# A GELU MLP on one core: the order of a small copy and the turning of a bias on VectorE

## The chip, the cores and the metric

The kernel runs on one core of a Trainium2 chip. The metric is the device time of one execution in microseconds (us). A profile of one execution is a little shorter than that time (93.8 us against 95.05 us for the profiled run of the kernel before); its span runs from the first recorded instruction to the last. Engines are named as in the profile: PE is TensorE's matmuls, PEld its weight loads, DVE is VectorE, ACT ScalarE, POOL GpSimd, SP SyncE.

## The reference

```python
B, S, D, F = 1, 2048, 448, 1792          # all tensors bf16
h = einsum("bsd,df->bsf", x, w1) + b1
h = gelu(h, approximate=True)
out = einsum("bsf,fd->bsd", h, w2) + b2
```

The contraction of layer 1 has 448 = 3 x 128 + 64 rows. The last 64, the remainder rows, are the subject here.

## The kernel before

Every matmul of the two layers uses 64 of the 128 rows of the array, upper half or lower half by turns, and the halves work side by side. A pair of output tiles (`lo` = 0 and 1) goes through part a (three blocks, 64 rows of each) and part b (the other 64 rows of these blocks, then the remainder). In the last step of part b, tile 0 uses the upper half and tile 1 the lower, so the remainder rows of w1 of every odd tile must lie in the lower 64 partitions. The DMA brings them to the upper ones, and an engine copies them down. A helper records every operation and puts the semaphore waits that its list `after` names. The bias b1 arrives as 14 rows of 128 and is turned by VectorE, with four transposes and a cast (a copy into another type).

```python
RCUTS = (0, 4, 14)            # remainder rows come as tiles 0-3, then 4-13
def turn_b1():
    for q in range(4):
        pr.op("vector", ... e.transpose(b1t[32*q:32*q+32, :], b1n[:, 32*q:32*q+32]) ...)
    pr.op("vector", ... e.tensor_copy(b1_f, b1t[:, 0:NFT]) ..., event="b1")
...
# Layer1.step, k == KT (the remainder):
lhsT = w1r[rows, ft*P:(ft+1)*P]
after = [("w1r" if half else "w1rU", int(ft >= RCUTS[1]))]   # half 0 needs the copy
...
L[0].a(0, HC)
turn_rest()                   # TensorE turns the rest of x, VectorE and ScalarE copy it out
turn_b1()
for i in (0, 1):
    odd = ...                 # the odd tiles' columns of block i
    pr.op("vector", ... e.tensor_copy(odd(slice(0, H)), odd(slice(H, P))),
          after=[("w1r", i)], event=("w1rU", i))
L[1].a(0, HC); L[0].a(HC, SC); L[1].a(HC, SC)
L[0].b(); L[1].b(); L[2].a()
for j in range(3, NPAIR):
    L[j].a(); L[j - 1].b()
```

The gelu of a pair, on ScalarE, needs the turned bias and empties the pair's PSUM unit (PSUM is the memory that holds the sums of the matmuls). There are four units, so the fifth pair of layer 1 waits for the gelus of the first.

Of the kernel before, what the change touches and what calls it, by code (L numbers as in the profile page):

```python
# [73 lines left out]
def bass_standalone__dense_activation_gelu__prompt_kernel(  # L74
# [23 lines left out]
    with ExitStack() as es:  # L98
# [80 lines left out]
        def turn_b1():  # L179
            for q in range(4):  # L180
                pr.op("vector", lambda e, q=q: e.transpose(  # L181
                    b1t[32 * q:32 * q + 32, :], b1n[:, 32 * q:32 * q + 32]), after=["b1n"], event=("b1t", q))
            pr.op("vector", lambda e: e.tensor_copy(b1_f[:, :], b1t[:, 0:NFT]),  # L183
                  after=[("b1t", q) for q in range(4)], event="b1")
# [187 lines left out]
        def turn_rest():  # L372


            turn_block(1, 2, 2, 0, [("xT0", 0, 2)])
            for q in range(STC // 2):
                turn(lambda half, q=q: spot(2, 1)[:, half, q, :], lambda rows, q=q: xr[rows, q, :], ("xr", q), ["xr_in"])
            drain_blocks("vector", 1, (2,), 2, ("xr", 1))
            for src, engine in enumerate(("vector", "scalar")):
                i = spot(2, 1, HALVES[src])  # L380
                for dst in (src, 1 - src):
                    o = xT[HALVES[dst], KT, 0:SC].rearrange("p (q two b s) -> p b q two s", q=2, two=2, b=2)[:, :, :, src, :]
                    pr.op(engine, lambda e, o=o, i=i, engine=engine:
                          e.copy(o, i) if engine == "scalar" else e.tensor_copy(o, i),  # L384
                          after=[("xr", 1), ("xT0", 1, 2)], event=("xR0", dst, src))
            busy[(2, 1)] = ("xR0", 1, 0)
            busy[(2, 2)] = ("xR0", 0, 1)
# [4 lines left out]
        L = [Layer1(0, j) for j in range(NPAIR)]  # L392
        L[0].a(0, HC)
        turn_rest()
        turn_b1()

        for i in (0, 1):
            odd = lambda rows, i=i: w1r[rows, RCUTS[i] * P:RCUTS[i + 1] * P].rearrange(
                "p (j two q) -> p j two q", two=2, q=P)[:, :, 1, :]
            pr.op("vector", lambda e, odd=odd: e.tensor_copy(odd(slice(0, H)), odd(slice(H, P))),  # L400
                  after=[("w1r", i)], event=("w1rU", i))
        L[1].a(0, HC)
        L[0].a(HC, SC)
        L[1].a(HC, SC)
# [70 lines left out]
```

## Time and profile before

| | before |
|---|---|
| time, median of 3 runs (range) | 94.79 us (94.73 to 94.97) |
| span of the profile | 93.8 us |
| TensorE busy | 90.0 us, 96% |
| VectorE busy | 13.4 us, 14% |
| TensorE idle for the copy of remainder rows | 0.64 us as shown |

The rows of the profile that carry these are in the prediction below. Read such a profile in this order: which engine the chain that ended last runs through, where that chain leaves the engine, and then the timeline of each engine around that place.

### The profile page before, as it was taken

The page shows a single profiled execution, that of the slowest core. Times are in us where ns is not written, and L with a number is a line of the kernel's source. Part 1 is how long each engine was busy: PE and PEld are TensorE (multiplying, and loading weights), DVE is VectorE, ACT ScalarE, POOL GpSimd, SP SyncE. Part 2 cuts the span into 40 slices and gives each one's busy share as a digit, 9 for nine tenths or more (in the row PEclk, how much of TensorE's full clock was granted, in tenths as well). Part 3 has the DMA queues.
Part 4 walks back from the last instruction along what each step waited for, and adds up shares of the span by engine and source line. Part 5 has one row for each costly group of instructions (what it writes and reads, how often), then busy time and mean ns, then how long its engine had stood idle before and what let it go on. Part 6 is the DMA issues. An engine that isn't in the chain of part 4 may idle for free.

```text
span 93.8 us, 2086 instructions
## 1 busy us (share of the span) xinstructions
PE 90.0 (96%) x945; PEld 50.3 (54%) x945; DVE 13.4 (14%) x34; ACT 38.5 (41%) x64; POOL 1.7 (2%) x8
## 2 busy tenths in 40 slices
PE   6997999999999999999999999999999999999990
PEld 2382444566664444566654444566654444576990
DVE  0156001100234000000235000000134000000421
ACT  6065687900002887900001878900001878910001
POOL 6000000000000000000000000000000000000000
PEclk9999999999999999999999999999999999999999
DMA  2999999745564000000033000000022000000022
GB/s 47 347 278 323 380 294 114 130 102 119 73 136 155 0 0 7 0 0 0 0 99 104 0 3 0 7 0 0 0 98 98 7 0 0 0 0 7 24 74 98
DMA packets 12744, 7.32 MB, mean 78 GB/s; under 512 B 6976, under 2 KB 12544, under 8 KB 12736
## 3 DMA queue, kind: packets, MB, share of 16 engines
q1 hardware_dynamic: 11904, 6.80, 29.6%
q10 hardware_dynamic: 800, 0.39, 1.4%
q8 instruction: 7, 0.11, 0.5%
q14 instruction: 1, 0.01, 0.0%
q0 software_dynamic: 32, 0.00, 0.0%
HBM read 3.79 MB, written 1.84 MB: 60 GB/s over the span
## 4 chain that ended last, share of the span: by engine, by line
PE 94%; DVE 2%; issue 1%; ACT 0%; DVEq 0%
PE u L217 89%; PE u L192 4%; PE u L344 1%; DVE b1t L181 1%; DVE xT L384 1%; ACT out_sb L329 0%; DVE xT L357 0%; DVE w1r L400 0%; DVE b_f L183 0%; DVEq L63 0%
## 5 line engine op out<-in xcount | busy, mean ns | idle before, releaser
L269 ACT ACTIVATE g<-u,b_f 128x512 bf16<-128x512 f32 x56 | 35.0, 684 | 40.0 <-PE u L217 38.9
L217 PE MATMUL u<-w_sb,g 64*128 64x448 bf16 (+1 forms) x504 | 43.9, 328 | 0.0
L217 PE MATMUL u<-xT,w_sb 64*128 64x512 bf16 (+1 forms) x348 | 43.5, 371 | 0.1
L217 PEld LDWEIGHTS u<-w_sb,g 64*128 64x128 bf16 x504 | 28.7, 94 | 14.1
L217 PEld LDWEIGHTS u<-xT,w_sb 64*128 64x128 bf16 x348 | 19.5, 95 | 19.1 <-DMA w_sb<-in_w_dram 0.2
L217 PE MATMUL u<-xT,w1r 64*128 64x512 bf16 x56 | 16.7, 376 | 0.6 <-DVE w1r L400 0.6
L312 DVE TENSOR_TENSOR out_sb<-u,b_bc 128x448 bf16<-128x448 f32 x14 | 8.1, 620 | 61.3 <-PE u L217 61.3
L217 PEld LDWEIGHTS u<-xT,w1r 64*128 64x128 bf16 x56 | 5.3, 94 | 4.5 <-DVE w1r L400 1.1
L329 ACT CAST out_sb<-u 128x224 bf16<-128x224 f32 x1 | 0.3, 345 | 9.3 <-PE u L217 9.3
L192 PE MATMUL u<-const-bfloat16-1.0 128*128 128x512 bf16 (+1 forms) x8 | 3.4, 601 | 0.8 <-PEq L460 0.8
L192 PEld LDWEIGHTS u<-const-bfloat16-1.0 128*128 128x128 bf16 x8 | 1.0, 140 | 2.4 <-issue 2.4
L357 ACT COPY xT<-u 128x256 bf16<-128x256 bf16 x3 | 1.0, 374 | 2.5 <-PE u L344 2.5
L175 ACT ACT_TABLE_LOAD x1 | 1.3, 1283 | 0.7 <-PEq L460 0.7
L344 PEld LDWEIGHTS u<-ident,xn 64*128 64x128 bf16 x24 | 0.9, 127 | 0.9 <-issue 0.8
L187 DVE COPY xT<-xT 64x512 bf16<-64x512 bf16 x3 | 0.9, 289 | 3.4 <-DMA xT<-in_x_dram 3.3
L344 PE MATMUL u<-ident,xn 64*128 64x64 bf16 x24 | 1.1, 238 | 0.1
L423 DVE COPY b_z<-b_bc 1x448 bf16<-1x448 bf16 x1 | 0.3, 268 | 5.8 <-DMA b_bc<-in_b_dram 5.8
L384 ACT COPY xT<-u 64x256 bf16<-64x256 bf16 x2 | 0.7, 368 | 0.9 <-DVE xT L357 0.8
L357 DVE COPY xT<-u 128x256 bf16<-128x256 bf16 x3 | 0.8, 292 | 1.2 <-PE u L344 1.2
L320 DVE TENSOR_TENSOR out_sb<-u,b_bc 128x448 bf16<-128x448 f32 x1 | 0.6, 625 | 1.8 <-PE u L217 1.8
L181 DVE STREAM_TRANSPOSE b1t<-b1n 32x32 bf16<-32x32 bf16 x4 | 0.8, 202 | 0.1
L362 DVE COPY xr<-xn 128x256 bf16<-128x256 bf16 x1 | 0.2, 227 | 3.2 <-DMA xn<-in_x_dram 3.2
(18 smaller groups left out, 4.8 us busy)
## 6 DMA issues: line engine op xcount, KB each, us to landing
out_dram<-out_sb SPq DMA_DIRECT2D x16, 112.0 KB, 1.7
w_sb<-in_w_dram SPq DMA_DIRECT2D x2, 784.0 KB, 8.3
w_sb<-in_w_dram SPq DMA_DIRECT2D x1, 576.0 KB, 6.0
xn<-in_x_dram SPq DMA_DIRECT2D x1, 448.0 KB, 3.4
w_sb<-in_w_dram ACTq DMA_DIRECT2D x2, 192.0 KB, 4.1
w_sb<-in_w_dram SPq DMA_DIRECT2D x1, 384.0 KB, 4.5
xT<-in_x_dram SPq DMA_TRANSPOSE x12, 3.8
w1r<-in_w_dram SPq DMA_DIRECT2D x1, 160.0 KB, 4.8
```

What stands on the lines that cost most here:

```text
L175: pr.op("scalar", lambda e: e.activation(junk[:, :], one, ACT.Gelu_apprx_tanh), event="table")
L181: pr.op("vector", lambda e, q=q: e.transpose(b1t[32 * q:32 * q + 32, :], b1n[:, 32 * q:32 * q + 32]), after=["b1n"], event=("b1t", q))
L187: pr.op("vector", lambda e: e.tensor_copy(xT[0:H, KT, s0:s1], xT[H:P, KT, s0:s1]), after=after, event=event)
L192: pr.op("tensor", lambda e: e.matmul(unit[0][:, 0, 0:cols], lhsT=ones_w, rhs=ones_m[:, 0:cols], start=True, stop=True))
L217: o = pr.op("tensor", lambda e: e.matmul(unit[u][:, lo, cols], lhsT=lhsT, rhs=rhs, start=start, stop=stop, skip_group_check=skip), after=a ...
L269: pr.op("scalar", lambda e, lo=lo, ft=ft: e.activation(g[:, ft, c * SC:(c + 1) * SC], unit[u][:, lo, :], ACT.Gelu_apprx_tanh, bias=b1_f[:, ...
L312: pr.op("vector", lambda e, lo=lo, j=j: e.tensor_tensor(out=out_sb[:, j, :], in0=unit[u][:, lo, 0:D], in1=b2_bc[:, :], op=ALU.add), after= ...
L320: pr.op("vector", lambda e: e.tensor_tensor(out=out_sb[:, j, :].rearrange("p (two h) -> p two h", two=2), in0=unit[u][:, :, 0:DH], in1=b2_ ...
L329: pr.op("scalar", lambda e: e.copy(out_sb[:, j, DH:D], unit[u][:, 1, 0:DH]), after=[y[1]], event=("o", j, 1))
L344: pr.op("tensor", lambda e, half=half, rows=rows: e.transpose(o(half), i(rows), ident[rows, rows]), after=["ident"] + after, event=event i ...
L357: pr.op(engine, lambda e, i=i: (e.copy if engine == "scalar" else e.tensor_copy)(o[:, i], f[:, i]), after=[wait or ("xt", h, ks[-1])], eve ...
L384: e.copy(o, i) if engine == "scalar" else e.tensor_copy(o, i),
```

## The change

The first copy of remainder rows (tiles 0 to 3) goes ahead of the five instructions that turn the bias. The intent is that TensorE, which needs that copy first, waits for it no longer. The second copy stays last.

```diff
         L[0].a(0, HC)
         turn_rest()
-        turn_b1()
 
         for i in (0, 1):
             ...
             pr.op("vector", lambda e, odd=odd: e.tensor_copy(odd(slice(0, H)), odd(slice(H, P))),
                   after=[("w1r", i)], event=("w1rU", i))
+            if i == 0:
+                turn_b1()
```

## The prediction

> **What bounds the kernel now.** I read the page first (busy shares, then the chain that ended last), then the chain in order of time, then the timeline of each engine around the one gap in it.
>
> ```profile
> PE 90.0 (96%) x945; PEld 50.3 (54%) x945; DVE 13.4 (14%) x34; ACT 38.5 (41%) x64; POOL 1.7 (2%) x8
> PE 94%; DVE 2%; issue 1%; ACT 0%; DVEq 0%
> ```
>
> TensorE (PE) sets the time: 94% of the chain that ended last is its matmuls. VectorE (DVE) is busy for 14% of the span but holds 2% of that chain, about 2 us, so there is one place where TensorE waits for it. The chain in order of time says where (start us, length us, what):
>
> ```profile
> 6.75 0.28 DVE xT L384
> 7.03 0.03 issue
> 7.07 0.20 DVE b1t L181
> ...
> 7.76 0.22 DVE b1t L181
> ...
> 8.10 0.18 DVE b_f L183
> 8.27 0.03 issue
> 8.30 0.23 DVE w1r L400
> 8.54 0.05 issue
> 8.59 82.99 PE u L217 x868
> ```
>
> From 6.11 to 8.54 us the chain runs through VectorE alone: it finishes turning x (L384), transposes the bias (L181, four times), casts it (L183), and only then copies the first remainder rows of w1 to the lower 64 partitions (L400). From 8.59 on the chain is one unbroken run of 868 matmuls up to the last output. So whatever moves the point 8.59 forward moves the end, unless a later wait appears in that run. What TensorE did meanwhile (two answers of the timeline, matmuls and weight loads, start, length, shapes, idle before and releaser):
>
> ```profile
> 7.57 0.38 PE L217 MATMUL u<-xT,w1r 64*128 64x512 bf16 x1
> 8.59 0.39 PE L217 MATMUL u<-xT,w1r 64*128 64x512 bf16 x1 [0.64 <-DVE w1r L400]
> 7.36 0.09 PEld L217 LDWEIGHTS u<-xT,w1r 64*128 64x128 bf16 x1
> 8.58 0.09 PEld L217 LDWEIGHTS u<-xT,w1r 64*128 64x128 bf16 x1 [1.13 <-DVE w1r L400]
> ```
>
> The first matmul on the remainder rows reads the rows as the DMA left them (upper half) and runs at 7.57. Its partner reads the copied rows (lower half) and runs at 8.59, released by the copy. The idle time of 0.64 us is only from the modelled end of one matmul to the start of the next; the loss in the rhythm of starts is larger, as worked out below.
>
> **What the Trainium skill says.** (1) "TensorEngine Tiling (Array Packing)", section Key Properties: tiles are independent, and different tiles can load weights and multiply in parallel. All matmuls here use 64 of 128 rows. The trace agrees: the groups of two remainder matmuls in layer 1 start at 11.40 and 12.91, and 14 matmuls lie between those points, so 1.51 / 14 = 0.108 us each, or one pair every 0.216 us. (2) "TensorE: Matmul & The Clock Gate", section Back-to-back issue gap, gives N/2.4 + 2.5 ns for the warm array, which is 216 ns for 512 columns; the pair rhythm just found is that, so two half-row streams each run at the full column rate. (3) "VectorE: DVE Perf Modes", section Two Vector instructions with no wait between them: an instruction whose inputs or output start in another group of 32 partitions than the ones before waits until every earlier one has finished. The trace agrees: L400's two copies, alike in partitions, overlap (0.22 + 0.35 us of work in 0.49 us), while the unlike neighbours in the chain above are 0.03 us apart. (4) "Perfetto Trace Analysis", section Tensor Engine Instruction: matmul ends in a profile are estimated. Hence I reckon with starts.
>
> **The change part by part.** Nothing is added or removed: five VectorE instructions of the bias (4 transposes, 1 cast) and one copy change places. In both orders the second copy (the other ten blocks of w1) comes last.
>
> The copy. After the last L384 ends at 7.03 it starts at about 7.06 and takes 0.23, so it is done at 7.29; with the 0.05 from copy to weight load that the chain shows, TensorE may go on at 7.34 instead of 8.58. Its own input landed long before: issued at 2.26, 3.7 us to landing, so 5.96.
>
> TensorE. Its pairs before the stop follow at 7.13, 7.35, 7.57, so the partner would have run beside the matmul at 7.57. ScalarE's last copy of x, which that partner needs too, ends at 6.49 + 0.76 = 7.25, also in time. So the partner moves from 8.59 to 7.57 or a hair later (its half of the array: 1.02 us earlier) and the next pair from 8.59 to 7.57 + 0.22 = 7.79 (the other half, whose first matmul of that pair now starts at 8.59: 0.80 us earlier). The half that gains only 0.80 is the later one from then on: before, one half was a matmul behind the other, afterwards they march level.
>
> The bias. It is ready not at 8.28 but one copy and one gap later, at 8.28 + 0.26 = 8.54. ScalarE's first gelu therefore starts at about 8.63 instead of 8.37.
>
> The second copy. It loses the overlap with the first and ends at about 8.57 + 0.35 = 8.92 instead of 8.79.
>
> The end. The last store waits for a VectorE sum (91.51 + 0.39 = 91.90) fed by the half that gains 0.80, and for a ScalarE copy (91.60 + 0.34 = 91.94) fed by the half that was a matmul behind. The first becomes 91.10; the second catches up and ends before it. So the store is released 91.94 - 91.10 = 0.84 us earlier. Sum: 94.79 - 0.84 = 93.95 us, or 0.9% less.
>
> **The rivals.**
>
> Rival 1, a later bias becomes the new wait. These rows are ScalarE's in the timeline:
>
> ```profile
> 8.37 2.56 ACT L269 ACTIVATE g<-u,b_f 128x512 bf16<-128x512 f32 x4 [1.11 <-DVE b_f L183]
> 11.82 1.26 ACT L269 ACTIVATE g<-u,b_f 128x512 bf16<-128x512 f32 x2 [0.89 <-PE u L217]
> ```
>
> ScalarE waits for the bias, and TensorE wants the four PSUM units back. The fifth pair of layer 1 takes the first unit again; it starts now at 8.59 + 14 pairs x 0.216 = 11.6, and will at 10.8. Its unit is free after two gelus, which begin at 8.63 and take 0.64 each in the row above, plus the tail of the last: 10.0. Slack 0.8 us. The four first gelus end at 11.19 instead of 10.93, and the third pair's, wanted by then at 11.0, is late by 0.2; a pair takes ScalarE 1.27 and TensorE 1.51, so ScalarE is level again one pair later. The 0.89 us that ScalarE idles before 11.82 speaks for this too. If I am wrong here, TensorE would stop at the fifth pair and the time would be between 94.0 and 94.8.
>
> Rival 2, a transfer takes the place of the wait. SyncE's issues in the timeline, and microseconds to landing from the list of DMA issues:
>
> ```profile
> 2.26 0.55 SPq L137 DMA_DIRECT2D w1r<-in_w_dram  x1
> 2.87 0.57 SPq L130 DMA_DIRECT2D w_sb<-in_w_dram  x1
> 3.48 0.50 SPq L137 DMA_DIRECT2D w1r<-in_w_dram  x1
> 4.02 0.59 SPq L130 DMA_DIRECT2D w_sb<-in_w_dram  x1
> ```
>
> ```profile
> w_sb<-in_w_dram SPq DMA_DIRECT2D x1, 576.0 KB, 6.0
> w_sb<-in_w_dram SPq DMA_DIRECT2D x1, 384.0 KB, 4.5
> w1r<-in_w_dram SPq DMA_DIRECT2D x1, 160.0 KB, 4.8
> w1r<-in_w_dram SPq DMA_DIRECT2D x1, 64.0 KB, 3.7
> ```
>
> The 384 KB of w1 land at 2.87 + 4.5 = 7.4; the third pair wants them after 4 pairs of matmuls, at 7.79 + 4 x 0.216 = 8.65. The 576 KB land at 4.02 + 6.0 = 10.0; the fifth pair wants them at 10.8. The other remainder rows land at 8.3 and their copy ends at 8.92; they are wanted at about 10.6. w2 was issued from 4.65 with 8.3 us to landing, thus about 13 to 14.5, and layer 2 will want it at 16.2 instead of 17.02. No transfer is within 0.7 us of binding. The DMA is near full in this stretch, so a run in which the 576 KB are late by more than 0.8 would lose part of the gain: 94.1 to 94.6.
>
> Rival 3, only the size differs. If the end follows the 0.64 us of shown idle time, the time is 94.15; if it follows the half of the array that gains 1.02, it is 93.77. If the copy came a few hundredths too late for the slot at 7.57 (it has about 0.2 us), the partner would slip and the lag of one half would stay; still at least 0.6 us would be won.
>
> Rival 4, the clock. The page grants full speed in all 40 slices (row PEclk), the matmul at 7.57 lasts as long (0.38) as the later ones, so there is no slow clock that the pause causes and its removal would lift.
>
> **Range and chances.** 93.95 us is the sum; the other sizes span 93.77 to 94.15, and the three runs of before lie 0.24 us apart, so I take 93.70 to 94.25 for eight in ten. Faster by over 2% would need less than 92.9, a gain of 1.9 us, which is more than the whole wait: 1%. Slower by over 2% has no mechanism here: 1%. Within 2%: 98%.
>
> **What would show it.** In the changed profile: L400's first copy starts at 7.06 and the four transposes follow at 7.33; the wait of TensorE for DVE w1r L400 is gone from the list of waits; both matmuls on the remainder rows of the first pair start at 7.57 to 7.6; the unbroken run of matmuls starts before 8 us, and VectorE's share of the chain falls from 2% to about 1%; the first gelu starts near 8.63 after a wait of 1.4 for the bias; layer 2 begins near 16.2. I am wrong if TensorE shows a new wait for w_sb, for ScalarE or for the second copy between 8 and 14 us, or if the first gelu's delay is still seen at layer 2's start.

## The result, and the profile after

The changed kernel takes 94.15 us (median of 6 runs, 93.69 to 94.43); the kernel before, in the same rounds and those of its first measurement, 94.94 us (94.73 to 95.06). The ratio is 0.9915 with a 95% interval of 0.9886 to 0.9945, so the gain is 0.8%, some 0.81 us. Ratios here are the mean time of one kernel's fast runs over that of the other's fast runs of the same rounds, so not quite the ratio of the medians quoted. Every execution behind a ratio in this document was in the fast state.

The page of the changed kernel, the chain by engine and by line:

```profile
PE 92%; DMA 4%; DVE 1%; issue 0%
PE u L217 92%; DMA xn<-in_x_dram 4%; DVE out_sb L326 0%; PE u L344 0%; DVE xT L357 0%
```

The lines for the bias (b1t) and for the copy (w1r) are no longer in the chain. Its pieces in order of time show one run of matmuls to the end, now from 5.64 us instead of 8.59:

```profile
5.64 84.80 PE u L217 x903
90.44 0.38 DVE out_sb L326
```

VectorE's timeline: the copy (L399 now) follows directly on the last copies of x, then the bias, and the second copy waits for its transfer:

```profile
6.02 0.60 DVE L384 COPY xT<-u 64x256 bf16<-64x256 bf16 x2
6.66 0.22 DVE L399 COPY w1r<-w1r 64x256 bf16<-64x256 bf16 x1
6.91 0.90 DVE L181 STREAM_TRANSPOSE b1t<-b1n 32x32 bf16<-32x32 bf16 x4
7.95 0.18 DVE L183 CAST b_f<-b1t 128x14 f32<-128x14 bf16 x1
9.20 0.35 DVE L399 COPY w1r<-w1r 64x640 bf16<-64x640 bf16 x1 [1.07 <-DMA w1r<-in_w_dram]
```

TensorE's timeline: the two remainder matmuls of the first pair are now one group, both starting at 7.28, since the group lasts 0.38, which is the length of one. The next pair follows 0.22 us later, in the next slot (a slot is a pair's place in the rhythm of starts, 0.216 us long):

```profile
7.28 0.38 PE L217 MATMUL u<-xT,w1r 64*128 64x512 bf16 x2
7.50 0.81 PE L217 MATMUL u<-xT,w_sb 64*128 64x512 bf16 x6
```

The span falls by 93.8 - 92.6 = 1.2 us, more than the time does. The part of it that the change did not make can be read off: VectorE was done with x at 6.02 + 0.60 = 6.62 in this execution and at 7.03 in the one of before, with the same instructions up to there. What that is, the second traces show.

### The profile page after: what moved, and what is told of

Same layout as the page of the kernel before. It is cut to its first block, busy times and chain, and to the rows that moved or that the text cites. A ratio compares the mean times of both kernels' runs of the same rounds, so it can differ in the third digit from the quotient of the medians.

```text
span 92.6 us, 2086 instructions
## 1 busy us (share of the span) xinstructions
PE 89.1 (96%) x945; PEld 45.6 (49%) x945; DVE 13.5 (15%) x34; ACT 38.4 (41%) x64; POOL 1.7 (2%) x8
## 4 chain that ended last, share of the span: by engine, by line
PE 92%; DMA 4%; DVE 1%; issue 0%
PE u L217 92%; DMA xn<-in_x_dram 4%; DVE out_sb L326 0%; PE u L344 0%; DVE xT L357 0%
## 5 line engine op out<-in xcount | busy, mean ns | idle before, releaser
L217 PE MATMUL u<-w_sb,g 64*128 64x448 bf16 (+1 forms) x504 | 43.2, 328 | 0.0
L217 PE MATMUL u<-xT,w_sb 64*128 64x512 bf16 (+1 forms) x348 | 41.0, 369 | 0.3 <-DVE xT L357 0.2
L217 PEld LDWEIGHTS u<-w_sb,g 64*128 64x128 bf16 x504 | 24.5, 94 | 18.4
L217 PEld LDWEIGHTS u<-xT,w_sb 64*128 64x128 bf16 x348 | 16.7, 94 | 19.6 <-DMA w_sb<-in_w_dram 1.0
L217 PE MATMUL u<-xT,w1r 64*128 64x512 bf16 x56 | 10.6, 376 | 0.0
L217 PEld LDWEIGHTS u<-xT,w1r 64*128 64x128 bf16 x56 | 2.7, 94 | 3.3
L192 PE MATMUL u<-const-bfloat16-1.0 128*128 128x512 bf16 (+1 forms) x8 | 3.2, 577 | 0.8 <-PEq L461 0.8
L192 PEld LDWEIGHTS u<-const-bfloat16-1.0 128*128 128x128 bf16 x8 | 1.0, 137 | 2.4 <-issue 2.4
L399 DVE COPY w1r<-w1r 64x256 bf16<-64x256 bf16 (+1 forms) x2 | 0.6, 289 | 1.1 <-DMA w1r<-in_w_dram 1.1
```

The costliest lines, as they stand in the source:

```text
L192: pr.op("tensor", lambda e: e.matmul(unit[0][:, 0, 0:cols], lhsT=ones_w, rhs=ones_m[:, 0:cols], start=True, stop=True))
L217: o = pr.op("tensor", lambda e: e.matmul(unit[u][:, lo, cols], lhsT=lhsT, rhs=rhs, start=start, stop=stop, skip_group_check=skip), after=a ...
L399: pr.op("vector", lambda e, odd=odd: e.tensor_copy(odd(slice(0, H)), odd(slice(H, P))), after=[("w1r", i)], event=("w1rU", i))
```

## The experiments

All gave correct results. In the tables "before" is the kernel before in the same rounds.

| run | what | median us | before us | ratio (95%) |
|---|---|---|---|---|
| again | the changed kernel | 93.97 | 94.93 | 0.9908 (0.9874 to 0.9942) |
| fine_after | changed, last block of w1 in two transfers | 93.85 | 94.93 | 0.9908 (0.9876 to 0.9939) |
| fine_before | before, with that split | 94.62 | 94.93 | 0.9982 (0.9952 to 1.0012) |
| pool_copy | before, first copy on GpSimd | 93.97 | 94.93 | 0.9920 (0.9884 to 0.9957) |
| copy_mid | copy after two transposes | 94.09 | 94.67 | 0.9933 (0.9905 to 0.9961) |
| copy_k4 | copy after four transposes, ahead of the cast | 94.45 | 94.67 | 0.9978 (0.9956 to 1.0000) |
| bias_last | both copies ahead of the bias | 95.16 | 94.67 | 1.0043 (1.0006 to 1.0081) |
| delay6 | changed, bias 1.3 us later | 94.33 | 94.67 | 0.9956 (0.9931 to 0.9981) |

Four more were single looks, for their traces: copy_k3 (94.61 us), copy_mid_again (94.05), before_again (94.44) and after_third (93.74), with a single run of the kernel before at 94.84. Single runs have no known state and carry no verdict, and none is drawn from their times.

My theory was that the whole gain is TensorE's wait for the copy, and that the bias and the transfers have room to spare. The rivals: the later bias is what moves the time; the transfers of w1 are the new wait; TensorE waits as a whole rather than half by half.

### The copy on another engine, the bias where it was (pool_copy)

```diff
-            pr.op("vector", lambda e, odd=odd: e.tensor_copy(...),
-                  after=[("w1r", i)], event=("w1rU", i))
+            pr.op("gpsimd" if i == 0 else "vector", lambda e, odd=odd: e.tensor_copy(...),
+                  after=[("w1r", i)] + (["ident", "b2z0"] if i == 0 else []), event=("w1rU", i))
```

The added waits are on GpSimd's own earlier instructions. The author added them because the check for races refused the kernel without them; the record keeps no trace of that refusal.

> The kernel before, with the first copy of remainder rows done by GpSimd, which is idle from 2.5 us on, in place of VectorE; the bias stays first on VectorE. My theory (TensorE waited for the copy, whatever engine makes it, and the delay of the bias neither helps nor hurts): if GpSimd is done with it by 7.5 us, the gain is that of the changed kernel, ratio 0.991 to 0.992, with ScalarE's first gelu at about 8.1 to 8.3 as in the kernel before less one copy. Rival (the later bias is what changed the time, by moving ScalarE's work): no gain from this kernel, ratio 0.998 to 1.002. If GpSimd takes over 1.5 us for the copy, the gain is smaller by what it is late.

GpSimd's timeline, and then TensorE's at the first pair:

```profile
5.92 0.39 POOL L400 COPY w1r<-w1r 64x256 bf16<-64x256 bf16 x1 [3.44 <-DMA w1r<-in_w_dram]
```

```profile
7.21 0.38 PE L217 MATMUL u<-xT,w1r 64*128 64x512 bf16 x2
```

The copy is done at 6.31, the two remainder matmuls again start together, and the ratio is that of the changed kernel (0.9920 against 0.9915 and 0.9908). The bias is ready at 7.93 and ScalarE's first gelu starts at 8.03, without the copy in front. So the gain is the copy's coming in time, on either engine, and it needs no move of the bias. A copy done 0.9 us ahead of its use, as here, gains nothing over one done 0.4 us ahead, as in the changed kernel.

### How late the copy may be (copy_mid, copy_k4, copy_k3, copy_mid_again)

```diff
         turn_rest()
+        turn_b1(range(n), False)          # n = 2, 3 or 4 transposes, no cast
         for i in (0, 1):
             ...
             if i == 0:
-                turn_b1()
+                turn_b1(range(n, 4))      # the rest, and the cast
```

> The changed kernel with the copy after two of the four transposes of the bias. The copy is then done 0.46 us later, at about 7.75 in the clock of the profile of before, 0.2 us after the slot of its matmul. My theory (two half-row streams; only the half that needs the copy slips, the other half's next matmul waits no longer than about 7.80 against 7.79): one half falls a matmul behind again but the end moves by at most 0.05 us, ratio 0.991 to 0.993. Rival (TensorE as a whole waits for the copy from the moment the first matmul of its pair starts): 0.2 us of the gain lost, ratio 0.993 to 0.995.

> The changed kernel with the copy after all four transposes but ahead of the cast. The copy is done about 8.24 and TensorE goes on at about 8.29 in place of 8.59 in the kernel before. My theory: 0.30 us less than before, ratio 0.996 to 0.998, and TensorE again shows a wait for the copy, of 0.7 to 0.8 us for its weight load. Rival (the order alone matters, or the bias's cast): either the full gain, 0.991 to 0.992, or none.

> The changed kernel with the copy after three of the four transposes; one look for the trace. From VectorE's last copy of x to TensorE's release the chain should be 3 x 0.233 + 0.25 + 0.05 = 1.0 us; the slot of the partner matmul lay 0.5 to 0.9 us after that copy in the traces so far. My theory (two half-row streams): the partner starts at the release, 0.1 to 0.5 us after its slot, while the next matmul of the other half starts at the later of the release and 0.22 us after the slot; from that next matmul to the last drain it is 83.35 us, as in the kernel before, and not 83.29, as in the changed kernel, since one half is a matmul behind. Rival (both halves wait alike): the next pair starts 0.22 us after the late partner.

> The kernel with the copy after two transposes again, one look: in its first trace TensorE's slow clock lasted until 6.6 us and its slot came so late (0.95 us after VectorE's last copy of x) that the copy was in time, and the run told nothing. If the clock rises earlier this time, the slot is 0.5 to 0.7 us after that copy, the release 0.77 after it, the partner 0.1 to 0.25 us late, and the other half's next matmul not late at all or by less than 0.05 (my theory); the rival has it late by as much as the partner.

With four transposes ahead, the wait is back. The chain of copy_k4:

```profile
7.44 0.23 DVE w1r L401
7.67 0.05 issue
7.72 82.99 PE u L218 x868
```

From VectorE's last copy of x (its end at 6.47) to the release at 7.72 it is 1.25 us, against 1.56 in the kernel before (7.03 to 8.59): the 0.31 us that the cast and the waits before it cost, which is the expected 0.30. The time agrees (ratio 0.9978, within the 0.996 to 0.998 expected).

The first run of copy_mid told nothing. TensorE itself was slow in its trace: the first remainder matmul started only 0.95 us after the last copy of x, at 7.85, so the copy, done at 7.62, was in time. Its ratio of 0.9933 has an interval that holds both theories. The second look caught the case. TensorE's timeline of copy_mid_again, and then that of copy_k3:

```profile
7.30 0.64 PE L218 MATMUL u<-xT,w1r 64*128 64x512 bf16 x2
7.56 1.03 PE L218 MATMUL u<-xT,w_sb 64*128 64x512 bf16 x6
```

```profile
7.65 0.87 PE L218 MATMUL u<-xT,w1r 64*128 64x512 bf16 x2
8.13 0.60 PE L218 MATMUL u<-xT,w_sb 64*128 64x512 bf16 x3
```

A group of two lasts from the start of the first to the end of the second, so the partner starts 0.64 - 0.38 = 0.26 us after the first matmul in copy_mid_again and 0.87 - 0.38 = 0.49 after it in copy_k3. The next matmul, on the other half, starts at the same moment as the late partner, not a slot of 0.22 us behind it. In copy_mid_again it is therefore at 7.56 where it would have been at 7.30 + 0.22 = 7.52: the partner lost 0.26 us, the other half 0.04. The rival of a TensorE that waits as a whole would have put it at 7.78. The halves are two streams, but they start in the order of TensorE's one list: the next matmul needs nothing of the copy, and in all six traces with a late partner it starts 3 or 4 ns after that partner, never ahead of it. So the other half loses what the partner is late, less one slot: 0.04 us of 0.26 here, 0.27 of 0.49 in copy_k3, and 0.80 of 1.02 in the kernel before. That is why a copy which one half alone needs held up both. From that next matmul to the last drain (the copy of the last sums out of PSUM) copy_k3 took 83.35 us, as expected of a kernel with one half behind.

### How late the bias may be (delay6, bias_last)

```diff
             if i == 0:
+                for q in range(6):        # delay6: into a buffer that nothing reads
+                    pr.op("vector", ... e.transpose(b1d[...], b1n[...]) ...)
                 turn_b1()
```

```diff
-            if i == 0:
-                turn_b1()
+        turn_b1()                         # bias_last: after the loop
```

> The changed kernel with six more transposes of the bias into a buffer that nothing reads, between the copy and the bias: 6 x 0.233 = 1.4 us more, so that the bias is ready at about 9.9 in the clock of before (9.35 in that of the changed kernel's profile), and the first pair's gelus end at 11.4 (10.75). My theory (0.8 us of slack): TensorE waits for the PSUM unit ahead of the fifth pair and loses 0.4 to 0.6 us against the changed kernel, ratio 0.995 to 0.998. If the slack is larger than 1.4, ratio 0.991 to 0.992; if there is none, 1.004 to 1.007.

> The changed kernel with the bias after both copies. The second copy waits for its transfer, which landed at 8.3 in the trace of before and at 9.2 in that of the changed kernel, so the bias is ready only at about 9.9 to 10.8 and the first pair's two gelus end at 11.3 to 12.1. My theory (bias has 0.8 us of slack and no more, since the fifth pair of layer 1 wants the first PSUM unit back at 10.6 to 10.8): TensorE waits for ScalarE there, and 0.5 to 1.5 us are lost against the changed kernel: ratio 0.997 to 1.007. Rival (the time of the bias does not matter at all): ratio 0.991 to 0.992.

The chain of delay6 at the place that the expectation named:

```profile
9.33 1.28 ACT g L270 x2
10.60 0.14 issue
10.74 79.89 PE u L218 x849
```

TensorE's remainder matmuls of the third pair started at 10.06, so the fifth pair's turn was at 10.06 + 0.22 = 10.28, and it started at 10.74: 0.46 us lost, where 0.4 to 0.6 was expected. By the times, 0.9956 against the changed kernel's 0.9908 to 0.9915 is 0.4 to 0.5% of 94.7 us, again 0.4 to 0.5 us; but those ratios come from other rounds and their intervals overlap, so it is the trace that shows the loss. In this trace the bias could have come 0.46 us sooner than 9.24, so at 8.78, without loss; in the changed order without the 1.3 us it would have been ready at about 7.95. That is the 0.8 us of room that the prediction reckoned.

In bias_last the second copy waits for its transfer (landing at 8.77), the bias comes at 10.38, and TensorE's row for the fifth pair reads:

```profile
11.89 0.61 PE L217 MATMUL u<-xT,w_sb 64*128 64x512 bf16 x4 [1.36 <-ACT g L269]
```

Its turn was at 10.15 + 0.22 = 10.37, so 1.52 us are lost, and the kernel is slower than the one before (1.0043). So the 0.25 us by which the changed order delays the bias lie within its room, and a delay of more than 0.8 us does not.

### The transfers (again, fine_after, fine_before)

```diff
-        W1CUTS = (0, 2, 4, 8, 14)
+        W1CUTS = (0, 2, 4, 8, 10, 14)
...
         load_w1(3)
+        load_w1(4)
```

> The changed kernel itself, once more, for a second trace and a tighter interval. My theory (the whole gain is that TensorE no longer waits for the copy of the first remainder rows): 0.80 to 0.84 us less than before, a ratio of 0.991 to 0.992, and no wait of TensorE for the copy. Rival (transfers of w1 are the new wait in many runs, so that part of the gain is lost and the times scatter): 0.3 to 0.7 us less, ratio 0.993 to 0.997, and a wait of TensorE for the 384 KB or the 576 KB of w1 of more than 0.1 us in the trace.

> The changed kernel with the last block of w1 (tiles 8 to 13) loaded as two transfers, tiles 8 and 9 first, so that the fifth pair's weights land about 1 us earlier. If the transfers cost the changed kernel nothing on average (my theory): the same time as the changed kernel within 0.1 us, ratio to before 0.990 to 0.993. If the landing of this block has become the wait in many runs (rival): up to 0.3 us faster than the changed kernel and a smaller scatter, ratio 0.987 to 0.989.

> The kernel before with that same split of the last block of w1. Here TensorE wants the fifth pair's weights about 0.8 us later, so neither theory expects a gain: ratio 0.997 to 1.003. A gain as large as in the run of the split on the changed kernel would say that the split helps for another reason than the one under test.

The first trace of the changed kernel showed weight loads that waited for a transfer (PEld, with idle time before and releaser):

```profile
8.33 1.64 PEld L217 LDWEIGHTS u<-xT,w_sb 64*128 64x128 bf16 x18 [0.30 <-DMA w_sb<-in_w_dram]
10.55 0.55 PEld L217 LDWEIGHTS u<-xT,w_sb 64*128 64x128 bf16 x8 [0.36 <-DMA w_sb<-in_w_dram]
```

Most of that idle time is not TensorE's: a weight load runs ahead of its matmul (the one at 7.36 in the kernel before belongs to the matmul at 7.57). The first matmul behind the second wait started at 10.56, and its turn was at 10.30 + 0.22 = 10.52, so 0.04 us were lost; behind the first wait nothing was.

But the 576 KB of w1 landed at 10.51 there, in the very slot in which they were wanted, where the prediction had 0.8 us of room. In the other traces of that order they landed at 10.39 (again) and 9.73 (after_third), and were wanted 14 slots of 0.216 us after the pair behind the first remainder matmuls, so at 8.05 + 3.02 = 11.07 and 7.35 + 3.02 = 10.37, in time. In copy_mid_again, too, they were close: they landed at 10.62, wanted at 7.56 + 3.02 = 10.58, and the fifth pair started at 10.67, 0.08 us late. Splitting that block, with its first part landing at 8.66, left the ratio at 0.9908 in the same rounds as the 0.9908 of the unsplit kernel. So on average the transfers cost nothing that these runs can show, though single executions touch them. fine_before is 0.9982 with an interval that holds 1.

### Where the size of the gain comes from (before_again, after_third)

The kernels are the two under study, unchanged.

> The kernel before once more, for a second trace. My theory: whatever the moment at which TensorE's clock rises, TensorE is released 1.55 us after VectorE's last copy of x (7.04 to 8.59 in its first trace), because the five bias instructions and the copy stand between; and from there to the last drain it is 83.35 us. The absolute times may shift by up to 0.5 us with that moment.

> The changed kernel once more, for a third trace. My theory: no wait of TensorE for the copy at any moment of the clock's rise, the pair after the first remainder pair 0.22 us behind it, 83.29 us from there to the last drain; the slot itself lies wherever the clock puts it, between 7.0 us (rise before 4.5) and 7.9 us (rise at 6.6).

The chain of before_again:

```profile
6.12 0.28 DVE xT L384
...
7.96 82.99 PE u L217 x868
```

VectorE ended its last copy of x at 6.40 here and at 7.03 in the first trace, and TensorE was released 1.56 us later in both. The shift goes with TensorE's speed. The row of its 256-column matmuls between 4.8 and 6.5 us (count, busy us, mean ns of one), for the first trace of before, for before_again and for again:

```profile
L217 PE MATMUL u<-xT,w_sb 64*128 64x256 bf16 x18 | 1.7, 321 | 0.1
```

```profile
L217 PE MATMUL u<-xT,w_sb 64*128 64x256 bf16 x24 | 1.7, 270 | 0.3 <-DVE xT L357 0.2
```

```profile
L217 PE MATMUL u<-xT,w_sb 64*128 64x256 bf16 x14 | 1.9, 406 | 0.1
```

One such matmul takes 414 ns while the array is slow and 269 ns once it is fast; the last slow weight load was at 5.9 us in the first trace, before 4 us in the second, at 6.6 in the third. VectorE's last copy of x ended at 6.40 to 6.62 us in the six traces with a rise before 4.5 us, and at 6.69 to 7.12 in the eight others. The Trainium skill, "TensorE: Matmul & The Clock Gate", section What's actually happening, says that the clock rises after a busy window that runs freely, so that its moment differs from run to run. These traces agree that it differs; they do not show the window itself.

This moment weighs differently on the two kernels. Before, TensorE was released 1.56 us after the last copy of x, whatever its own speed. Changed, the pair behind the first remainder matmuls starts as soon as TensorE has worked off its earlier matmuls: 0.87 and 0.86 us after the last copy of x where the clock rose early (after, after_third), 0.91 where it rose at 6.2 (fine_after), 1.11 where it rose at 6.6 (again). With the rise at 5.9, as in the trace on which the prediction rests, the slot at 7.57 puts it at 0.76. All fourteen traces can be read so, since none of the runs changes the instructions ahead of that slot (where the pair itself was held, as before, take one slot after the first remainder matmul). They give 0.74 to 1.17 us, 0.86 on average, so the change moves that pair by 0.39 to 0.82 us, 0.70 on average, by the moment of the rise.

From that pair to the last drain it is 83.35 us in both traces of before (91.60 + 0.34 - 8.59; 90.97 + 0.35 - 7.96 is 83.36 by the rounded rows), 83.28 and 83.29 us in after_third and again, and 83.32 in the first trace of the changed kernel (90.44 + 0.38 - 7.50), whose fifth pair lost 0.04 to a transfer. This is the half that was a matmul behind and no longer is: about 0.07 us. Together the traces put the gain at an estimated 0.77 us on average, from 0.46 to 0.89 in single executions.

## Why the prediction was right

**The bound and the place.** TensorE's stream of matmuls sets the end, and the gap behind the first remainder matmul was the one place to win. Right: the wait is gone and pool_copy wins the same without touching the bias.

**The copy.** Predicted to follow the last copy of x by 0.03 us, to take 0.23 and to be in time. It followed by 0.04, took 0.22, and was done at 6.88 against a slot at 7.28. The absolute times are 0.3 to 0.4 us earlier than predicted, in an execution in which the clock rose before 4 us and not at 5.9.

**TensorE, half by half.** Predicted 1.02 us for one half and 0.80 for the other, the 0.80 deciding. The level halves are in the trace, and copy_mid_again shows the two streams apart. The prediction reckoned with starts and not with the shown idle time of 0.64 us. The traces bear that out: in pool_copy, whose slot lay 0.52 us after the last copy of x (0.54 in the first trace of before), the next pair came 0.74 us after that copy and not 1.56, so 0.82 sooner. The times alone do not, since the interval of the gain, 0.52 to 1.08 us, holds 0.64 too.

**The bias.** The wait of ScalarE was predicted as 1.4 us and is 1.37 in its row:

```profile
8.21 3.77 ACT L269 ACTIVATE g<-u,b_f 128x512 bf16<-128x512 f32 x6 [1.37 <-DVE b_f L183]
```

Six gelus in one run instead of four come of both shifts: ScalarE starts later, and TensorE has the third pair ready sooner, which together use up the 0.89 us that ScalarE idled before. The room of 0.8 us was confirmed by delay6, so rival 1 was rightly set aside.

**The end and the sum.** Predicted 0.84 us less. Measured 0.8 to 0.9% of 94.9 us in two independent sets of rounds, which is 0.81 and 0.87 us. The absolute 93.95 was missed by 0.2 us (94.15; 93.97 in the second set), of which 0.15 is that the kernel before read 94.94 and not 94.79 once it had six runs.

**What was off.** Rival 2 was sized too safely: "No transfer is within 0.7 us of binding" took one execution's landings for all. The 576 KB landed 6.0 us after issue there and 6.5 in the changed trace, and the room was gone in that execution; the 384 KB landed at 8.29 for a pair at 8.36, where 7.4 and 8.65 were predicted. The second copy was predicted to end at 8.92 and ended at 9.55, as its transfer came later; nobody needed it before 10.3. Rival 4 spoke of full speed in all 40 slices; that row shows no throttle, yet the array ran its early matmuls in 414 ns where later ones take 269, and by the moment of the rise the gain of a single execution goes from about 0.46 to 0.89 us. The 0.84 was read from a trace near the upper end of that span, so it was partly luck that the number came out so close. The fourteen traces put the mean at about 0.77 us and the times at 0.81 and 0.87; their intervals hold all of these, and which is right stays open. Last, "all matmuls" in the prediction leaves out the eight on constants at the start (L192), which use 128 rows; nothing rests on that.

## What to carry to other kernels

When several engines feed the one that sets the time, put its next need first in each feeder's queue, and give what has room the later place: here 0.25 us of bias for 0.8 us of TensorE. Then stop: a copy still earlier won nothing, and moving the second copy ahead too cost 1.5 us in its trace, because it waits for a transfer and a queue makes everything behind it wait as well. Measure slack in more than one execution, since the landing of the 576 KB moved by 0.9 us here (9.73 to 10.62), and the clock's rise moved the slot by 0.4 us against the copies of x.

## What the Trainium skill lacked or had wrong

- "TensorE: Matmul & The Clock Gate", section What you observe, gives the rise of the clock at around 4 us of sustained activity, within 500 ns from run to run. Here matmuls run from 0.78 us on, and the last slow weight load lay before 4 us in some traces and at 5.9 and 6.6 us in others, so the spread is at least 2.4 us. (The packed traces also hold clock records: in nine of the fourteen full clock is on record only from 3.7 to 6.0 us on; the other five hold no record.) The work in between holds transposes and short waits, so it is not quite the page's case.
- No page says that a row of granted clock can miss this rise, though one warns that recorded clock events can be unreliable. The row read 1.00 in every window from 0.8 to 8 us while the same matmul took 414 and then 269 ns. The clock record of that trace of before begins at 6.01 us, and the row counts unrecorded time as full clock.
- "TensorEngine Tiling (Array Packing)", section Key Properties, says that tiles are independent, but not what that means behind a wait: with the partner 0.26 and 0.49 us late, the other half lost 0.04 and 0.27 us (the lateness less one slot), and a half once behind stayed a matmul behind to the end (83.35 against 83.28 us) unless a later wait let it catch up, as the fifth pair's did in copy_mid_again.
